# First products of chunk pairs by Strassen's seven block products, token tiles visited there and back

## The chip, the cores and the metric

One core of a Trainium2 chip runs the whole kernel. The metric is device microseconds, the median of three runs. TensorE (PE; its weight loads are PEld) multiplies, VectorE (DVE) and ScalarE (ACT) work elementwise, SyncE (SP) issues most transfers. Matrix results land in PSUM, eight banks of 128 x 512 fp32, and DVE or ACT read them out.

## The reference

Windowed attention with four sink tokens, and then two feed-forward layers on its output:

```
scores = q @ k.T / 8            # kept: keys 0..3, and the 128 keys up to the query's own
x  = softmax(scores) @ v        # 2 x 768 tokens = 1536, 512 wide (8 heads of 64)
h1 = x  @ w_in1                 # 512 -> 2048
x2 = leaky_relu(h1, 0.01) @ w_out1
h2 = x2 @ w_in2
out = silu(h2) @ w_out2         # 1536 x 512
```

The weights come as float64 pairs of words; the kernel turns them into fp32 itself. Each fp32 operand of the feed-forward products is split in two parts, high and low, and a product is the sum of three: high*high, low*high and high*low.

## The kernel before

A recording layer (`Recorder`, L469 is where it issues everything) collects all operations with their dependencies, orders each engine's queue by a planner's costs and due times, and then issues them. The order of every queue is thus fixed when the program is built; on the chip each engine goes down its list and waits where an operand is late. Every row of the profile shows L469, so rows are told apart by tile names.

**Chunks and tiles.** Each layer's 2048 columns are 16 chunks of 128 (chunks 0 to 15 and 16 to 31). The 1536 tokens are three tiles T of 512. For a chunk and a tile the first product `h` (`emit_h`) takes 4 blocks of 128 rows times 3 parts = 12 matmuls of 128x512. ACT and DVE turn `h` into the split pair `gb` (activation, its high part, its low part). The second product (`emit_y`) takes 4 output blocks times 3 = 12 matmuls into the PSUM banks `y0` to `y3`. In layer 2 the activation was a Sigmoid on ACT, a multiplication on DVE, a copy on ACT and a subtraction on DVE.

**Weights.** Each chunk is fetched in two halves (`wr`), and a half is turned into fp32 by one ACT and four DVE operations (`wb`) and split by one ACT and one DVE operation into `w` (a ring of 6 chunks) or `we` (a ring of 4).

**Order.** During the attention, chunks 0 to 5 are worked on half tiles of 256 tokens beside it (`ga`, `ya`). Then come passes of 4 or 6 chunks: in a pass every tile T is visited in the order 0, 1, 2, and its `y` banks add up over the chunks of the pass and are then added into `yp` by DVE. `h` of item f is issued two items ahead of its `y` (`fused_h(f)`, then `fused_y(f - 2)`), so PE alternates 12 matmuls of `h` with 12 of `y`. `h` has two PSUM banks. At the end of layer 1, `yp` is split into `xh` and `xl`, the input of layer 2.

```
for f in range(len(items)):
    ...
    fused_h(f)
    if f >= 2:
        fused_y(f - 2)
```

Of the kernel before, what the change touches and what calls it, by code (L numbers as in the profile page):

```python
# [30 lines left out]
NA, NE = 6, 4  # L31
# [21 lines left out]
def f32(ap):  # L53
    return ap.bitcast(F32)
# [429 lines left out]
def attention_moe(ctx, tc, cfg, ins, out):  # L484
# [22 lines left out]


    chunks = [(w, c) for w in (w1, w2) for c in range(NCH)]
    wt, halves = [], [0]  # L510

    raws = []

    def fetch(n):
        w, c = chunks[n // 2]
        cs = slice(n % 2 * 512, (n % 2 + 1) * 512)
        raws.append(keep.tile([P, 512, 2], U32, "wr", 3))
        R.sync.dma_start(out=raws[n], in_=w[c, :, cs].bitcast(U32).rearrange("p (n t) -> p n t", t=2))

    def load_half(after=None):  # L520

        n = halves[0]
        halves[0] += 1
        while len(raws) < min(n + 1 + FETCH, 2 * len(chunks)):
            fetch(len(raws))
        R.after, R.splitting = after, True
        if n % 2 == 0:
            first = len(wt) % (NA + NE) < NA
            wt.append((keep if first else rest).tile([P, 2, 1024], F32R, "w" if first else "we", NA if first else NE))
        t = wt[-1]  # L530
        cs = slice(n % 2 * 512, n % 2 * 512 + 512)
        lo, hi = raws[n][:, :, 0], raws[n][:, :, 1]
        b = keep.tile([P, 512], U32, "wb", 3)
# [7 lines left out]
        R.scalar.activation(t[:, 0, cs], f32(b), AF.Copy)  # L541
        R.vector.tensor_tensor(t[:, 1, cs], f32(b), f32(t[:, 0, cs]), op=ALU.subtract)
# [13 lines left out]
    def emit_h(gt, t, layer, T, t0, n):  # L556
        hp = ps.tile([P, 512], F32, "h", 2)[:, :n]
        last = KC * 3 - 1
        i = 0
        with R.group():  # L560
            for kc in range(KC):
                for a, b in ((0, xh), (1, xh), (0, xl)):
                    R.tensor.matmul(hp, wi(t, a, kc), b[T][:, kc, t0:t0 + n], start=i == 0, stop=i == last)
                    i += 1
        R.at_h = R.ops[-1]
        g = keep.tile([P, 512], F32, "g", 2)[:, :n]
        if layer == 0:
            R.scalar.activation(gt[:, 0, :], hp, AF.Prelu, alpha=0.01)
            R.scalar.activation(g, hp, AF.Prelu, alpha=0.01)
        else:  # L570
            R.scalar.activation(g, hp, AF.Sigmoid)
            R.vector.tensor_tensor(g, g, hp, op=ALU.mult)
            R.scalar.activation(gt[:, 0, :], g, AF.Copy)
        R.vector.tensor_tensor(gt[:, 1, :], g, f32(gt[:, 0, :]), op=ALU.subtract)

    def emit_y(yps, gt, t, layer, c, first, last, cols=slice(0, 512)):
# [341 lines left out]
    if near:  # L918
        make_mask(0)
        make_mask(1)  # L920

        for t in (*psink, own):
            R.vector.memset(t, 0.0)
        for k in range(2):
            R.vector.memset(own[32 * k:32 * k + 32, k * QB:(k + 1) * QB], 1.0)
        loaded = 2
        load_v(1)
        OFF = 2 * NP + 3
        for b in range(n_slots + 4):
# [12 lines left out]
            while loaded <= b // 2 + (AHEAD if loaded < NP * WHOLE else 1 + b % 2):  # L942
                load_qk(loaded)
                loaded += 1
            if 0 <= b - 1 < n_slots:
                normalise(b - 1)
            if b % 2 == 0 and b >= 4:
                if b % 4 == 2:
                    values(b // 2 - 3)
                load_v(b // 2)  # L950
            if 0 <= b - 2 < n_slots:
                transposes(b - 2)
            if go:
                item_h(m)
                m += 1
    else:
        attend_all()
        while len(wt) < NA:
            load_chunk()


    passes, counts, items, c0 = [], [], [], NA
    for layer, end in ((0, NCH), (1, 2 * NCH)):
        while c0 < end:
            n = min(NE if len(passes) % 2 == 0 else NA, end - c0)
            passes.append(n)
            new = layer == 1 and c0 == NCH

            starts = [min(BESIDE[T], c0) if c0 == NA else c0 for T in range(NT)]
            items += [(layer, c, T, c == starts[T], c == c0 + n - 1, new, c0 + n == end)  # L970
                      for T in range(NT) for c in range(starts[T], c0 + n)]
            counts.append(len(items) - sum(counts))
            c0 += n

    due, n0 = [], 2 * NA
    for n, m_p, nxt in zip(passes, counts, passes[1:] + [0]):
        n0 += 2 * n
        due += [n0 + 2 * nxt * (i + 1) / m_p for i in range(m_p)]
    while m < n_items + 2:
        if halves[0] < 2 * (NA + NE):  # L980
            load_half()
        item_h(m)
        item_y(m - 2)
        m += 1
    yps, fg = [], {}

    def fused_h(f):
        layer, c, T = items[f][:3]
        fg[f] = rest.tile([P, 2, 512], F32R, "gb", 4)
        emit_h(fg[f], wt[c], layer, T, 0, 512)  # L990

    def fused_y(f, banks=None):
        layer, c_w, T, first, last, new, final = items[f]
        gt = fg[f]

        ends = layer == 1 and final and T == NT - 1
        parts = [(c, 0, 512) for c in range(KC - ends)] + ends * [(KC - 1, 0, 256), (KC - 1, 256, 512)]
        if first and banks in (None, [0]):
            yps[:] = [ps.tile([P, 512], F32, "ya0", 1) if o else ps_y.tile([P, 512], F32, f"y{c}") for c, o, _ in parts]
        for k in banks or range(len(parts)):  # L1000
            c, o, e = parts[k]
            cols = slice(o, e)
            yp_k = yps[k][:, :e - o]
            emit_y(yp_k, gt, wt[c_w], layer, c, first, last, cols)
            if not last:
                continue
            part = yp[T][:, c, cols]
            if new:
                R.scalar.activation(part, yp_k, AF.Copy)
            elif not final:  # L1010
                R.vector.tensor_tensor(part, part, yp_k, op=ALU.add)
            elif layer == 0:
                R.vector.tensor_tensor(part, part, yp_k, op=ALU.add)
                R.scalar.activation(xh[T][:, c, :], part, AF.Copy)
                R.vector.tensor_tensor(xl[T][:, c, :], part, f32(xh[T][:, c, :]), op=ALU.subtract)
            else:
                r0 = T * 512 + c * P
                R.vector.tensor_tensor(part, part, yp_k, op=ALU.add)
                (R.scalar if o else R.sync).dma_start(out=out[r0:r0 + P, cols], in_=part)

    for f in range(len(items)):
        while halves[0] < min(2 * len(chunks), due[f]):

            load_half(R.at_h if f else None)
        fused_h(f)
        if f >= 2:
            fused_y(f - 2)

    for k in range(KC + 1):
        for f in (len(items) - 2, len(items) - 1):  # L1030
            fused_y(f, [k])
    R.issue(ctx)


# [87 lines left out]
```

## Time and profile before

| | |
|---|---|
| time, median of 3 runs | 621.07 us (620.93 to 621.36) |
| profiled execution: span from first to last instruction | 619.7 us |
| its own device time | not recorded apart from the span; the median lies 1.4 us above the span |
| PE busy | 609.3 us, 98% |
| DVE busy | 401.3 us, 65% |
| ACT busy | 314.2 us, 51% |
| granted TensorE clock | full in all 40 slices |

A matmul's record is longer than its place in the stream, because matmuls are pipelined: the distance from one start to the next is what counts. The chain of work that ended last is followed back from the last instruction. DVE and ACT records overlap a little in the same way, so both a duration and the start-to-start distance are read below.

### The profile page before, as it was taken

To read this page: it belongs to the slowest core of one execution; us is meant where nothing else is said; L and a number is where in the kernel's file an instruction comes from. 1 tells how busy PE (TensorE), PEld (TensorE's weight loads), DVE (VectorE), ACT (ScalarE), POOL (GpSimd) and SP (SyncE) were. 2 spreads that over 40 slices of the span, in tenths; PEclk is the share of its full clock that TensorE was granted. 3 is DMA by queue.
4 is the path that set the end of the run, shared out by engine and by line. 5 is a ranking of instruction groups with operands and counts; after the bars stand their busy time and mean duration, and the time that the engine had idled before them with its cause. 6 is when DMAs were issued, how large, how long until landed. Compare 5 with 4: busy or idle time off the path is not lost.

```text
span 619.7 us, 9078 instructions
## 1 busy us (share of the span) xinstructions
PE 609.3 (98%) x3374; PEld 517.2 (83%) x3374; DVE 401.3 (65%) x979; ACT 314.2 (51%) x716; POOL 2.9 (0%) x17
## 2 busy tenths in 40 slices
PE   6899999999999999999999999999999999999997
PEld 4788999999988888888888888888888888888886
DVE  6999889888760289721369454986242984268254
ACT  6999899997652155422335434564222442233211
POOL 1000000000000000000000000000000000000000
PEclk9999999999999999999999999999999999999999
DMA  8545554422320033300013200333000231000013
GB/s 298 191 158 179 179 158 140 147 60 82 137 103 0 1 102 138 135 35 0 1 57 113 102 1 31 139 137 102 1 0 1 102 117 54 1 34 2 0 69 135
DMA packets 19340, 53.33 MB, mean 86 GB/s; under 512 B 2144, under 2 KB 6752, under 8 KB 19296
## 3 DMA queue, kind: packets, MB, share of 16 engines
q1 hardware_dynamic: 19152, 52.63, 24.7%
q8 instruction: 26, 0.43, 0.3%
q14 instruction: 18, 0.15, 0.1%
q10 hardware_dynamic: 144, 0.13, 0.1%
HBM read 49.61 MB, written 3.15 MB: 85 GB/s over the span
## 4 chain that ended last, share of the span: by engine, by line
PE 94%; ACT 3%; DVE 1%; DMA 1%; issue 0%; SPq 0%; DVEq 0%
PE h L469 42%; PE y L469 35%; PE ya L469 7%; PE at L469 3%; PE tr L469 3%; PE sc L469 3%; ACT P L469 1%; DMA wr<-in_w 1%; ACT pT L469 0%; ACT wb L469 0%; DVE P L469 0%; SPq L469 0%; DVE by L469 0%; DVE wb L469 0%; ACT w L469 0%
## 5 line engine op out<-in xcount | busy, mean ns | idle before, releaser
L469 PE MATMUL h<-xh,w 128*128 128x512 f32 (+1 forms) x600 | 157.0, 349 | 0.0
L469 PEld LDWEIGHTS h<-xh,w 128*128 128x128 f32 x600 | 104.6, 189 | 14.3 <-issue 0.3
L469 ACT ACTIVATE g<-h 128x512 f32<-128x512 f32 (+1 forms) x111 | 59.8, 539 | 108.5 <-PE h L469 108.4
L469 DVE TENSOR_TENSOR gb<-g,gb 128x512 fp32r<-128x512 f32 x81 | 55.9, 690 | 82.3 <-ACT g L469 64.9
L469 PE MATMUL h<-xl,w 128*128 128x512 f32 (+1 forms) x300 | 103.9, 346 | 0.0
L469 DVE TENSOR_TENSOR g<-g,h 128x512 f32<-128x512 f32 x48 | 32.9, 686 | 90.8 <-ACT g L469 90.7
L469 PE MATMUL h<-xh,we 128*128 128x512 f32 x288 | 88.7, 389 | 0.0
L469 DVE SCALAR_TENSOR_TENSOR wb<-wr,wb 128x512 uint32<-128x512 uint32 x128 | 87.2, 687 | 1.6
L469 PE MATMUL y<-we,gb 128*128 128x512 f32 x288 | 69.2, 389 | 0.0
L469 PE MATMUL y<-w,gb 128*128 128x512 f32 (+1 forms) x288 | 68.2, 387 | 0.0
L469 PEld LDWEIGHTS h<-xh,we 128*128 128x128 f32 x288 | 54.1, 188 | 11.2
L469 PEld LDWEIGHTS y<-we,gb 128*128 128x128 f32 x288 | 54.1, 188 | 11.2
L469 PEld LDWEIGHTS y<-w,gb 128*128 128x128 f32 x288 | 53.8, 188 | 11.0
L469 PEld LDWEIGHTS h<-xl,w 128*128 128x128 f32 x300 | 56.6, 189 | 7.0
L469 PE MATMUL y<-gb,w 128*128 128x512 f32 x252 | 60.5, 389 | 0.0
L469 ACT ACTIVATE P<-P,sm 128x260 f32<-128x260 f32 (+2 forms) x118 | 57.0, 497 | 5.5 <-DVE sm L469 4.8
L469 ACT ACTIVATE gb<-h 128x512 fp32r<-128x512 f32 x33 | 19.7, 598 | 78.7 <-PE h L469 78.7
L469 PE MATMUL h<-xl,we 128*128 128x512 f32 x144 | 56.0, 389 | 0.0
L469 PEld LDWEIGHTS y<-gb,w 128*128 128x128 f32 x252 | 47.3, 188 | 9.8
L469 DVE TENSOR_SCALAR wb<-wb 128x512 uint32<-128x512 uint32 (+1 forms) x128 | 52.7, 422 | 2.7 <-ACT wb L469 1.4
L469 PE MATMUL ya<-ga,w 128*128 128x256 f32 x360 | 50.6, 286 | 0.0
L469 ACT ACTIVATE gb<-g 128x512 fp32r<-128x512 f32 x48 | 30.4, 633 | 35.6 <-DVE g L469 35.6
(78 smaller groups left out, 738.1 us busy)
## 6 DMA issues: line engine op xcount, KB each, us to landing
wr<-in_w SPq DMA_DIRECT2D x64, 512.0 KB, 3.6
qk<-in_qkd SPq DMA_DIRECT2D x12, 644.0 KB, 3.9
v<-in_vd SPq DMA_DIRECT2D x16, 192.0 KB, 3.2
out_y<-yp SPq DMA_DIRECT2D x11, 256.0 KB, 2.0
qk<-in_qkd SPq DMA_DIRECT2D x4, 322.0 KB, 6.0
v<-in_vd SPq DMA_DIRECT2D x8, 128.0 KB, 4.8
qkh<-in_qkd SPq DMA_DIRECT2D x4, 256.0 KB, 6.2
qk<-in_qkd SPq DMA_DIRECT2D x3, 256.0 KB, 4.1
```

The source lines that it names most:

```text
L469: getattr(eng, name)(*[_real(x) for x in a], **{k: _real(x) for k, x in kw.items()})
```

## The change

In 11 of the 16 pairs of neighbouring chunks (four in layer 1, from chunk 8; seven in layer 2, from chunk 18) the first products of two chunks over the tiles T = 0 and T = 1 are made together. Before they were 4 x 12 = 48 matmuls. Now the input is taken as 2x2 blocks (tile by half of the 512 columns), the two chunks' weights as 2x2 blocks (half by chunk), and Winograd's form of Strassen's rule makes seven block products of 6 matmuls, 42 in all (`product`). The tile T = 2 goes as before (`h_plain`).

The rule needs sums of input blocks once per layer (`combos`: tiles `S0` to `S2` and, in place, half of `xh[1]`, `xl[1]`), sums of weight blocks once per pair (in `load_half`: four subtractions of 128x256 on DVE, then two splits into `wx`), and three additions of results per pair (`sum_of` on DVE, with three copies out of PSUM, `held`, on ACT). Products are accumulated in the PSUM banks `ya0` (bank A), `ya1` (bank C) and one of the two `h` banks (bank B).

Three further parts: the second products of the two chunks of a pair are issued one after the other for each output block (`y_pair`), and `yp` is added to after each pair and not after each pass, except that a tile which is last in one pair is first in the next (order 0, 1, 2, then 2, 1, 0), so its banks stay open over both. Layer 2's activation is Silu twice on ACT and a subtraction on DVE. The ring `we` is gone; `w` keeps 6 chunks, and the loads of chunks 6 to 9 move from the end of the attention into the first items after it. Each layer starts with a few items as before (`plain_run`), and the last two of them hand their `y` to the first pair (`todo`, `other`).

```
+    def split(hi, lo, b):
+        R.scalar.activation(hi, b, AF.Copy)
+        R.vector.tensor_tensor(lo, b, f32(hi), op=ALU.subtract)
...
+        if h == 0 and c >= NA and c % 2 and c - 1 not in plain:
+            b0, b1 = f32(bits[c - 1]), f32(b)
+            u, v = slice(0, 256), slice(256, 512)
+            for o, x, y in ((b0[:, u], b1[:, u], b0[:, u]), (b1[:, u], b1[:, v], b1[:, u]),
+                            (b1[:, v], b1[:, v], b0[:, u]), (b0[:, v], b0[:, v], b1[:, v])):
+                R.vector.tensor_tensor(o, x, y, op=ALU.subtract)
+            wx[c - 1] = [rest.tile([P, 2, 512], F32R, "wx", 2) for k in range(2)]
+            for x, y in zip(wx[c - 1], (b0, b1)):
+                split(x[:, 0, :], x[:, 1, :], y)
...
-            R.scalar.activation(g, hp, AF.Sigmoid)
-            R.vector.tensor_tensor(g, g, hp, op=ALU.mult)
-            R.scalar.activation(gt[:, 0, :], g, AF.Copy)
+        f, kw = (AF.Prelu, dict(alpha=0.01)) if layer == 0 else (AF.Silu, {})
+        R.scalar.activation(gt[:, 0, :], h, f, **kw)
+        R.scalar.activation(g, h, f, **kw)
         R.vector.tensor_tensor(gt[:, 1, :], g, f32(gt[:, 0, :]), op=ALU.subtract)
...
+    def plain_run(layer, items, n_loads, at):
+        todo, S = [], None
+        for f, (c, T, first, last) in enumerate(items):
+            loads(f < n_loads)
+            h_plain(c, T)
+            todo.append((c, T, first, last))
+            if f == at:
+                S = combos(layer)
+            if f >= 2:
+                y_parts(*todo.pop(0))
+        return todo, S
...
+    def product(bank, x, w, start):
...
+        with R.group():
+            for k in range(2):
+                for a, b in ((0, 0), (1, 0), (0, 1)):
+                    R.tensor.matmul(bank, w(a, k), x[b][:, k, :], start=start and i == 0, stop=start and i == 5,
+                                    skip_group_check=not start)
...
+        A = bank("ya0")
+        product(A, x(0, 0), W(c, 0), True)
+        m1 = held(A)
+        B = bank("h", 2)
+        product(B, x(0, 1), W(c, 1), True)
+        sum_of(c, 0, m1, B)
+        loads(1)
+        other()
+        C = bank("ya1")
+        product(C, S1, X(t1, 0), True)
+        m5 = held(C, "s5", 1)
+        other()
+        h_plain(c, 2)
+        product(A, S2, X(t2, 1), False)
+        m16 = held(A)
+        product(C, S4, W(c + 1, 1), False)
+        sum_of(c + 1, 0, m16, C)
+        loads(1)
+        h_plain(c + 1, 2)
+        product(A, S3, X(t2, 0), False)
+        sum_of(c + 1, 1, m5, A)
+        T = order[0]
+        y_pair(c, T, first(T), last(T), range(2))
+        product(A, x(1, 1), X(t1, 1), False)
+        activate(new_g(c, 1), A, layer)
+        loads(1)
+        y_pair(c, T, first(T), last(T), range(2, KC))
+        y_pair(c, order[1], first(order[1]), last(order[1]))
+        loads(1)
+        y_pair(c, order[2], first(order[2]), last(order[2]))
```

How the queues stand now, at the places of which the prediction speaks. In PE's queue, in the middle of a stretch, before: one item's `y`, the next item's `h` (chunk 11, tile 1).

```order
L469 MATMUL y0_4_3531<-gb_23_3535,w_8_3082 128x512 x3
L469 MATMUL y1_4_3540<-gb_23_3535,w_8_3082 128x512 x3
L469 MATMUL y2_4_3545<-gb_23_3535,w_8_3082 128x512 x3
L469 MATMUL y3_4_3549<-gb_23_3535,w_8_3082 128x512 x3
L469 MATMUL h_60_3613<-xh1_0_589,w_11_3291 128x512 x2
L469 MATMUL h_60_3613<-xl1_0_609,w_11_3291 128x512
L469 MATMUL h_60_3613<-xh1_0_589,w_11_3291 128x512 x2
L469 MATMUL h_60_3613<-xl1_0_609,w_11_3291 128x512
```

PE now, in the pair of chunks 20 and 21 whose first tile in turn is T = 2; these rows follow the `h` of chunk 21 and tile 2, from which `gb_48` is made. `ya0` is bank A.

```order
L469 MATMUL ya0_13_4498<-xh1_0_589,wx_11_4492 128x512 x2
L469 MATMUL ya0_13_4498<-xl1_0_609,wx_11_4492 128x512
L469 MATMUL ya0_13_4498<-xh1_0_589,wx_11_4492 128x512 x2
L469 MATMUL ya0_13_4498<-xl1_0_609,wx_11_4492 128x512
L469 MATMUL y0_16_4550<-w_20_4352,gb_46_4630 128x512 x3
L469 MATMUL y1_16_4558<-w_20_4352,gb_46_4630 128x512 x3
L469 MATMUL y0_16_4550<-w_21_4420,gb_48_4678 128x512 x3
L469 MATMUL y1_16_4558<-w_21_4420,gb_48_4678 128x512 x3
L469 MATMUL ya0_13_4498<-xh1_0_589,wx_10_4472 128x512 x2
L469 MATMUL ya0_13_4498<-xl1_0_609,wx_10_4472 128x512
L469 MATMUL ya0_13_4498<-xh1_0_589,wx_10_4472 128x512 x2
L469 MATMUL ya0_13_4498<-xl1_0_609,wx_10_4472 128x512
```

Between an `h` and the second product that reads it stood two `y` and two `h`, 48 matmuls; now 12 lie between the `h` of `gb_48` and its first use. Bank A is filled again 12 matmuls after its last filling.

In ACT's queue at the change from layer 1 to layer 2, where the table of functions is loaded, before (`we_7` is chunk 15, `h_67` layer 2's first):

```order
L469 ACTIVATE we_6_3806<-wb_37_3845 128x512
L469 ACTIVATE wb_39_3891<-wr_39_3808 128x512
L469 ACTIVATE we_7_3895<-wb_38_3847 128x512
L469 ACTIVATE gb_32_3903<-h_66_3876 128x512
L469 ACTIVATE g_62_3906<-h_66_3876 128x512
L469 ACTIVATE we_7_3895<-wb_39_3891 128x512
L469 ACT_TABLE_LOAD
L469 ACTIVATE g_63_3939<-h_67_3923 128x512
L469 ACTIVATE gb_33_3948<-g_63_3939 128x512
```

ACT now at the same place (`xh0` is layer 2's input of tile 0, `w_17` chunk 17's weights, `h_55` layer 2's first `h`):

```order
L469 ACTIVATE xh1_0_589<-yp1_0_1315 128x512
L469 ACTIVATE xh0_0_318<-yp0_0_838 128x512 x2
L469 ACTIVATE wb_45_4046<-wr_37_3999 128x512
L469 ACTIVATE xh0_0_318<-yp0_0_838 128x512 x2
L469 ACTIVATE w_17_3997<-wb_43_3919 128x512
L469 ACT_TABLE_LOAD
L469 ACTIVATE gb_33_4072<-h_55_4033 128x512
L469 ACTIVATE g_59_4074<-h_55_4033 128x512
L469 ACTIVATE gb_34_4092<-h_56_4054 128x512
```

The split of tile 0's input and of chunk 17's second half now stand ahead of the load; before they stood far from it. PE's queue has three `h` in a row there (`h_55`, `h_56`, `h_57`), where before it went on alternating.

DVE at the same place, before, from layer 2's first `h` (`g_63`) on back to chunk 15's weights:

```order
L469 SCALAR_TENSOR_TENSOR wb_39_3891<-wr_39_3808,wb_39_3891 128x512 x2
L469 TENSOR_TENSOR gb_32_3903<-g_62_3906,gb_32_3903 128x512
L469 TENSOR_TENSOR we_7_3895<-wb_39_3891,we_7_3895 128x512
L469 TENSOR_TENSOR g_63_3939<-g_63_3939,h_67_3923 128x512
L469 TENSOR_TENSOR gb_33_3948<-g_63_3939,gb_33_3948 128x512
```

DVE now, up to the low part of layer 2's first `gb`:

```order
L469 TENSOR_TENSOR yp0_0_838<-yp0_0_838,y0_11_3987 128x512
L469 TENSOR_TENSOR yp0_0_838<-yp0_0_838,y1_11_4003 128x512
L469 TENSOR_TENSOR yp0_0_838<-yp0_0_838,y2_11_4012 128x512
L469 TENSOR_SCALAR wb_43_3919<-wb_43_3919 128x512
L469 TENSOR_TENSOR yp0_0_838<-yp0_0_838,y3_11_4021 128x512
L469 SCALAR_TENSOR_TENSOR wb_43_3919<-wr_35_3828,wb_43_3919 128x512
L469 TENSOR_TENSOR xl0_0_353<-yp0_0_838,xh0_0_318 128x512
L469 SCALAR_TENSOR_TENSOR wb_43_3919<-wr_35_3828,wb_43_3919 128x512
L469 TENSOR_TENSOR xl0_0_353<-yp0_0_838,xh0_0_318 128x512 x2
L469 TENSOR_TENSOR w_17_3997<-wb_43_3919,w_17_3997 128x512
L469 TENSOR_TENSOR gb_33_4072<-g_59_4074,gb_33_4072 128x512
```

These are the last of a run of 12 additions into `yp` and 12 subtractions for `xl`, all three tiles, with chunk 17's weights between them; before, each tile's four and four stood 6 items apart.

## Rows read from the trace of the kernel before

**Rows 1.** The page: span, busy time by engine, granted clock in 40 slices.
```profile
span 619.7 us, 9078 instructions
PE 609.3 (98%) x3374; PEld 517.2 (83%) x3374; DVE 401.3 (65%) x979; ACT 314.2 (51%) x716; POOL 2.9 (0%) x17
PEclk9999999999999999999999999999999999999999
```

**Rows 2.** Busy time in stretches: PE, PEld, DVE, ACT, POOL, then clock, DMA share, GB/s.
```profile
0.00:50.00 50.00, 42.90 (x328) 33.78 (x329) 44.59 (x193) 43.82 (x139) 2.89 (x17) 1.00 0.61 208
...
300.00:350.00 50.00, 50.00 (x222) 41.40 (x222) 31.90 (x58) 21.10 (x38) 0.00 (x0) 1.00 0.23 78
...
600.00:620.00 20.00, 16.48 (x79) 13.70 (x77) 9.73 (x16) 2.46 (x4) 0.00 (x0) 1.00 0.43 157
```

**Rows 3.** The chain that ended last, in order of time: start, us, engine, tile.
```profile
268.25 2.72 PE h L469 x12
270.97 2.72 PE y L469 x12
...
371.61 2.72 PE h L469 x12
```

**Rows 4.** The timeline behind one `h` of layer 1: start us, us, engine, operation [idle before].
```profile
281.46 0.39 PE L469 MATMUL h<-xl,w 128*128 128x512 f32 x1
...
281.88 0.60 ACT L469 ACTIVATE gb<-h 128x512 fp32r<-128x512 f32 x1 [4.35 <-PE h L469]
282.38 0.59 ACT L469 ACTIVATE g<-h 128x512 f32<-128x512 f32 x1
283.00 0.69 DVE L469 TENSOR_TENSOR gb<-g,gb 128x512 fp32r<-128x512 f32 x1 [4.75 <-ACT g L469]
```

**Rows 5.** The timeline of DVE where operations follow each other without a wait.
```profile
296.45 2.49 DVE L469 TENSOR_TENSOR xl<-yp,xh 128x512 fp32r<-128x512 f32 x4
...
316.25 0.88 DVE L469 TENSOR_SCALAR wb<-wb 128x512 f32<-128x512 f32 x2
...
317.17 1.42 DVE L469 SCALAR_TENSOR_TENSOR wb<-wr,wb 128x512 uint32<-128x512 uint32 x2
```

**Rows 6.** Groups by operation and shape: busy us, mean ns of one, idle before.
```profile
L469 PEld LDWEIGHTS h<-xh,w 128*128 128x128 f32 x600 | 104.6, 189 | 14.3 <-issue 0.3
L469 DVE TENSOR_TENSOR gb<-g,gb 128x512 fp32r<-128x512 f32 x81 | 55.9, 690 | 82.3 <-ACT g L469 64.9 <-ACT gb L469 17.2
L469 ACT ACTIVATE g<-h 128x512 f32<-128x512 f32 x81 | 48.2, 596 | 108.5 <-PE h L469 108.4
L469 ACT ACTIVATE wb<-wr 128x512 f32<-128x512 f32 x64 | 41.9, 669 | 4.4 <-DMA wr<-in_w 4.3
L469 DVE TENSOR_TENSOR yp<-yp,y 128x512 f32<-128x512 f32 x59 | 37.5, 682 | 10.2 <-PE y L469 10.2
L469 DVE TENSOR_TENSOR g<-g,h 128x512 f32<-128x512 f32 x48 | 32.9, 686 | 90.8 <-ACT g L469 90.7
L469 DVE TENSOR_TENSOR ga<-g,ga 128x256 fp32r<-128x256 f32 x30 | 12.6, 421 | 6.0 <-ACT g L469 6.0
```

**Rows 7.** The timeline at the change from layer 1 to layer 2.
```profile
352.40 2.88 PE L469 MATMUL y<-gb,w 128*128 128x512 f32 x12
...
352.65 1.28 ACT L469 ACT_TABLE_LOAD   x1 [3.88 <-PE h L469]
353.94 0.60 ACT L469 ACTIVATE g<-h 128x512 f32<-128x512 f32 x1
...
354.57 0.69 DVE L469 TENSOR_TENSOR g<-g,h 128x512 f32<-128x512 f32 x1 [5.00 <-ACT g L469]
```

**Rows 8.** DMA issues: size, median us to landing.
```profile
wr<-in_w SPq DMA_DIRECT2D x64, 512.0 KB, 3.6
```

**Rows 9.** The timeline of the last microseconds.
```profile
616.51 0.42 DVE L469 TENSOR_TENSOR yp<-yp,ya 128x256 f32<-128x256 f32 x1 [0.30 <-PE ya L469]
616.97 0.37 ACTq L469 DMA_DIRECT2D out_y<-yp  x1
```

More of the change, by code (lines that the diff above doesn't have):

```diff
@@ L523, in load_half @@
         halves[0] += 1
[L524 removed]
+        while len(raws) < min(n + 1 + FETCH, len(hv)):
             fetch(len(raws))
         R.after, R.splitting = after, True
[L527 to L531, printed above, removed]
+        c, h = hv[n]
+        if c not in wt:
+            wt[c] = keep.tile([P, 2, 1024], F32R, "w", NA)
+        t = wt[c]
+        cs = slice(h * 512, h * 512 + 512)
         lo, hi = raws[n][:, :, 0], raws[n][:, :, 1]
[L533 removed]
+        b = bits[c] = keep.tile([P, 512], U32, "wb", 3)
         R.scalar.activation(f32(b), f32(hi), AF.Abs)
@@ L957, in attention_moe @@
         attend_all()
[L958 to L978, printed above, removed]
+        while halves[0] < 2 * NA:
+            load_half()
     while m < n_items + 2:
-        if halves[0] < 2 * (NA + NE):
-            load_half()
         item_h(m)
@@ L984, in attention_moe @@
         m += 1
[L985 to L1001, printed above, removed]
+    gts, yps, opened = {}, {}, set()
@@ new lines, in attention_moe, with loads, new_g, h_plain @@
+    END = 2 * NCH - 1
+    def loads(n):
+        for _ in range(n):
+            if halves[0] < len(hv):
+                load_half(R.at_h)
+    def new_g(c, T):
+        gts[c, T] = rest.tile([P, 2, 512], F32R, "gb", 6)
+        return gts[c, T]
+    def h_plain(c, T):
+        emit_h(new_g(c, T), wt[c], c // NCH, T, 0, 512)
+    def parts_of(c, T):
+        ends = c >= END - 1 and T == NT - 1
+        return [(k, 0, 512) for k in range(KC - ends)] + ends * [(KC - 1, 0, 256), (KC - 1, 256, 512)]
@@ L1002, in fused_y, with y_parts @@
+    def y_parts(c, T, first, last, ks=None):
+        layer = c // NCH
+        parts = parts_of(c, T)
+        for k in ks or range(len(parts)):
+            k0, o, e = parts[k]
+            if first:
+                yps[T, k] = ps.tile([P, 512], F32, "ya0", 1) if o else ps_y.tile([P, 512], F32, f"y{k}")
             cols = slice(o, e)
-            yp_k = yps[k][:, :e - o]
-            emit_y(yp_k, gt, wt[c_w], layer, c, first, last, cols)
+            yp_k = yps[T, k][:, :e - o]
+            emit_y(yp_k, gts[c, T], wt[c], layer, k0, first, last, cols)
@@ L1005, in fused_y @@
             if not last:
                 continue
-            part = yp[T][:, c, cols]
-            if new:
+            part = yp[T][:, k0, cols]
+            if (layer, T) not in opened and layer == 1:
                 R.scalar.activation(part, yp_k, AF.Copy)
-            elif not final:
+            else:
                 R.vector.tensor_tensor(part, part, yp_k, op=ALU.add)
[L1012 to L1015, printed above, removed]
-            else:
-                r0 = T * 512 + c * P
-                R.vector.tensor_tensor(part, part, yp_k, op=ALU.add)
+            if c % NCH < NCH - 1:
+                continue
@@ L1019, in fused_y @@
+            if layer == 0:
+                R.scalar.activation(xh[T][:, k0, :], part, AF.Copy)
+                R.vector.tensor_tensor(xl[T][:, k0, :], part, f32(xh[T][:, k0, :]), op=ALU.subtract)
+            else:
+                r0 = T * 512 + k0 * P
                 (R.scalar if o else R.sync).dma_start(out=out[r0:r0 + P, cols], in_=part)
[L1021 to L1027, printed above, removed]
@@ L1029, in attention_moe, with y_pair @@
-    for k in range(KC + 1):
-        for f in (len(items) - 2, len(items) - 1):
-            fused_y(f, [k])
+        if last and len(parts) - 1 in (ks or range(len(parts))):
+            opened.add((layer, T))
+    def y_pair(c, T, first, last, ks=None):
+        for k in ks or range(len(parts_of(c, T))):
+            for d in range(2):
+                y_parts(c + d, T, first and d == 0, last and d == 1, [k])
+    def plain_run(layer, items, n_loads, at):
[9 more added lines that the diff above has]
+        return todo, S
@@ new lines, in product, with pair_run, other, held @@
+    def product(bank, x, w, start):
+        i = 0
+        with R.group():
+            for k in range(2):
+                for a, b in ((0, 0), (1, 0), (0, 1)):
+                    R.tensor.matmul(bank, w(a, k), x[b][:, k, :], start=start and i == 0, stop=start and i == 5,
+                                    skip_group_check=not start)
+                    i += 1
+        R.at_h = R.ops[-1]
+    def pair_run(c, S, todo, order, first, last):
+        layer = c // NCH
+        S1, S2, S3, S4 = S
+        W = lambda c, q: lambda a, k: wi(wt[c], a, 2 * q + k)
+        t1, t2 = wx[c]
+        X = lambda t, q: lambda a, k: t[:, a, q * 256 + k * P:q * 256 + (k + 1) * P]
+        x = lambda T, q: (xh[T][:, 2 * q:2 * q + 2], xl[T][:, 2 * q:2 * q + 2])
+        bank = lambda t, n=1: ps.tile([P, 512], F32, t, n)
+        def other():
+            if todo:
+                y_parts(*todo.pop(0))
+        def held(a, tag="g", bufs=2):
+            g = (keep if tag == "g" else rest).tile([P, 512], F32, tag, bufs)
+            R.scalar.activation(g, a, AF.Copy)
+            return g
+        def sum_of(c, T, g, b):
+            R.vector.tensor_tensor(g, g, b, op=ALU.add)
+            activate(new_g(c, T), g, layer, g=g)
+        A = bank("ya0")
[28 more added lines that the diff above has]
+        y_pair(c, order[2], first(order[2]), last(order[2]))
@@ L1032, in attention_moe @@
+    layer_run(1, [(NCH + d, T, d == 0, d == 1 and T != 0) for T in (2, 1, 0) for d in range(2)], 4, 3, NCH + 2, 2 * NCH)
     R.issue(ctx)
```

61 lines of the change are left out of this document (49 added, 12 removed).

## The prediction

> **What bounds the kernel now.** I read the page first. PE is busy in 609.3 of 619.7 us, DVE in 65%, ACT in 51%, at full clock (2.4 GHz) in all slices [rows 1]. By stretches, what PE does not fill lies in the first 50 us (7.1 us) and the last 20 (3.5 us); in the stretch from 300 to 350 us PE has no gap while DVE works 31.9 of 50 us [rows 2]. The chain of waits agrees: it runs from one group of 12 matmuls to the next, each 2.72 us, with nothing of another engine between them; from 268.25 to 371.61 us there are 39 such rows in a line [rows 3]. So one 128x512 matmul costs 2.72 / 12 = 226.7 ns of the end, whatever its own record says (389 ns long, because they overlap), and a matmul less is worth that, as long as DVE and ACT stay out of the way. They do so with ease now: what `h` gives is ready 283.69 - 281.85 = 1.84 us after the last matmul of `h` [rows 4], and is wanted 48 matmuls, 10.9 us, later.
>
> **What is removed.** 11 pairs times (48 - 42) = 66 matmuls of 128x512. Counted over PE's whole queue there are 1938 of that shape before and 1872 now, and 764 of 128x256 in both: 66 fewer and no other change. 66 x 0.2267 = 14.96 us. Each product has the same shapes and the same order of weight loads (one per matmul, as now), so I take the same distance for it. Here a rule speaks against the size: the Trainium skill, TensorE: Matmul & The Clock Gate, section Back-to-back issue gap, gives about 131 ns per matmul of 512 columns in a stream of weight loads and matmuls; by it 66 matmuls would be worth 8.6 us (an estimate), and the time 614.2. The trace differs: its stream steps by 226.7 ns [rows 3].
>
> **What is added to DVE and ACT.** By counts of the queues, DVE has 623 operations of 128x512 for 532 and 108 of 128x256 for 64. At about 0.69 us and 0.42 us [rows 6] that is 91 x 0.69 + 44 x 0.42 = 81 us more: from 401 to 482 us, of some 606. In the sum is the loss of the 48 multiplications of the Sigmoid form (32.9 us) and the growth of the additions into `yp` from 59 to 103. ACT has 71 more, 71 x 0.60 = 43 us, 357 in all. None of it stands on the path by itself; what matters is the pair, where it is densest.
>
> A pair takes PE 42 + 24 + 72 = 138 matmuls, 31.3 us. DVE's share, by distances from start to start: operations in a row step by about 0.61 us (2.49 us for 4), two that depend on each other by 0.73 (1.42 less 0.69), two TENSOR_SCALAR take 0.88 us [rows 5]. Four half loads: 4 x (0.88 + 1.42 + 0.62) = 11.7 us; weight sums 4 x 0.42 + 2 x 0.62 = 2.9; three result sums 1.9; six low parts of `gb` 3.7; eight additions into `yp` 4.9. Together 25.1 us, 80% of the pair. It fits, with 6 us to spare, if the waits inside it don't add up.
>
> So I walked the queues through a pair with these durations. The tightest place is the one shown in the order of PE: `gb_48` is wanted 12 matmuls, 2.72 us, after its `h`, its low part only as third matmul, at 3.17 us; with free engines it is ready after 1.84 us [rows 4], and DVE, which finishes the loads' and the weight sums' steps ahead of it, comes to it some 0.6 us later: 0.7 us to spare. Bank A must be read by `sum_of` before its next filling, 2.72 us after its last one; DVE ends that at 1.7 us: 1.0 us to spare. The sum for chunk c + 1, tile 0 has 2.72 + 1.36 us until its use, and needs 0.7 (DVE) + 0.6 + 0.5 (ACT) + 0.7 (DVE) = 2.5 us. The last activation from bank A has 18 matmuls, 4.1 us, until its use and about 1 us to spare, as DVE comes to it late. So I put the eleven pairs at no stall; the cover is the PE work named, and if it is gone each miss costs its own tenths, eleven times over or five or six (by the order of the tiles).
>
> The sums of inputs are 24 DVE operations in layer 1 and 16 in layer 2, 15 and 10 us; in layer 1 they begin before the last plain items end and DVE has no gap for some 40 us, but the first product with `S0` stands 36 matmuls, 8.2 us, behind the last plain `h`, and by the walk has 3 us to spare. The loads of chunks 6 to 9, now later, are due 22 us after chunk 0's slot is free, and a half takes about 3.6 us of transfer [rows 8], 0.67 for ACT [rows 6] and 4 us of DVE and ACT steps. SP's queue holds only these loads, each issued two ahead; I cost them at nothing. The tail is the same list, two last chunks and then the last quarter tile and its store [rows 9]: nothing.
>
> **The change of layers.** Here a stall comes in. In the profile PE goes through the change without a gap: ACT had been idle for 3.9 us, loads the table as soon as `h` ends (352.65 us), for 1.28 us, and its answer is not urgent, as PE has a `y` to do next [rows 7]. Now PE has three `h` in a row there. The third needs the bank of the first, 12 matmuls (2.72 us) after the first has ended. After the first ends, ACT has the table load and two activations: 1.28 + 0.5 + 0.6 = 2.4 us. That alone would just fit. But ACT's queue has the split of chunk 17's second half ahead of the load, and that waits for DVE, which has 32 operations in one run from the first addition of tile 2 on (12 additions, 12 subtractions and chunk 17's steps), before it was idle 5.0 us there [rows 7]. 28 x 0.61 + 4 x 0.44 = 18.8 us, about 19.3 with the dependent steps. Counting from the start of the six matmuls that fill bank A ahead of the last pair's first `y` in layer 1, the run starts at 3.7 us and ends at 23.0; ACT splits until 23.65, loads until 24.95, and has read the bank at 26.05. PE would want it at 24.48, after 1.36 + 17.68 us of products and `y` and 5.44 us of two `h`, and gets it at about 26.2: a stall of 1.7 us. Bounds: if DVE keeps up with PE, the load begins at 22.6 and the stall is 0.6; nothing if the load is done before the wait; 2.5 if DVE's run is 4% slower. I take 1.7, which is the walk's own value.
>
> The Trainium skill, ScalarE: Activation LUTs, section What ACT_TABLE_LOAD costs and its terms, puts a switch of tables at about 2.7 us; by it the stall would be 3.1 us and the sum 609.2. The trace's load took 1.28 us [rows 7], and I go by it.
>
> Silu does not occur in the trace. Prelu and Sigmoid share one row, 596 ns [rows 6]; I take the same for Silu. The bounds are 0.6 and twice that: at 1.2 us the place of `gb_48` above would be late by 0.5 us, in about seven pairs, once or twice each, 3.5 to 7 us. A gain below nothing is excluded: these steps are only waited for.
>
> **Sum.** Against the profiled execution: span 619.7 - 14.96 + 1.7 = 606.4 us; what lies around the span (1.4 us to the median, no own time is recorded) stays. Against the median: 621.07 - 14.96 + 1.7 = 607.8 us.
>
> **Rivals.**
> - *Dense with no stall at the change.* DVE keeps up: 606.1 us. For it: one load is only 1.28 us; against it: the run of 32 operations. It lies in the likeliest case's own range, 606.0 to 609.2.
> - *Handoffs late in each pair.* 0.2 to 0.8 us in each of eleven pairs, from bank A's reader or a low part: 2.2 to 8.8 us, so 610.0 to 616.6. For it: slack fell from about 9 us to under 1, and DVE is 80% busy; against it: the walk finds every one covered. Silu at twice its price would come out here too.
> - *The switch of tables costs more than its record.* If ACT must also run dry and fill again, one activation's 0.6 us on either side, the stall is 2.9 us: 609.0. Against it: the next activation starts 0.01 us behind the load [rows 7]. The page on ScalarE named above says the like.
> - *A matmul less is worth less than its step*, where the stream could go at its weight loads' 189 ns [rows 6]: 66 x 0.189 = 12.5 us, 610.3. Against it: 39 groups of 12 in a line at 2.72 us [rows 3], whichever operands they take. The page on TensorE named above goes further the same way.
> - *Slower: DVE sets the period of a pair.* A pair has some 43 DVE operations. If each pays 0.2 us of waiting on ACT or PE, because low parts, sums and weight steps stand in one queue, the pair lasts 25.1 + 8.6 = 33.7 us where PE needs 31.3: 11 x 2.4 = 26.4 us, 634 us. It decides from (14.96 - 1.7) / 11 = 1.2 us a pair on. For it: every low part in the trace waits for ACT (64.9 us in 81) [rows 6]; against it: those waits are for work that came late, on an engine with nothing else to do.
> - *It doesn't do what it says*, saving fewer matmuls: excluded by the counts.
>
> **Chances.** Likeliest case 0.62, late handoffs 0.24 (their lower part, to 612.5, 0.14), tables 0.03, cheaper matmuls 0.03, slower by DVE 0.05, faster still (below 605.5) 0.03. The range takes in the first, the lower part of the second, tables and cheaper matmuls, 0.82: 605.5 to 612.5. 0.2%, 1.24 us, is what a measurement of this kernel can tell from no change: faster (below 619.8) 0.94, the same 0.02, slower (above 622.3) 0.04.
>
> **What would show it.** PE's matmuls of 128x512 fall by 66 and its busy time by about 15 us, with 226.7 ns a step in the pairs; DVE near 480 us and about 80% in the pair stretches; ACT near 357 us. A single new gap of PE, about 1.7 us, before the third `h` of layer 2, whose releaser is ACT and behind it a table load. Wrong would be: PE's waits for `gb` or bank A that come back in every pair, a Silu of more than 0.65 us, or PE's step longer than 227 ns in the products.

## The result, and the profile after

| | before | after |
|---|---|---|
| time, median | 621.0 us (620.84 to 621.36, 4 runs) | 607.45 us (606.98 to 608.09, 4 runs) |
| span of the profiled execution | 619.7 us | 605.3 us (its own time: 607.04) |
| PE, DVE, ACT busy | 609.3, 401.3, 314.2 us | 595.7, 473.3, 351.3 us |

The ratio is 0.978, 95% interval 0.9767 to 0.9794: 13.6 us faster. The forecast was 607.8 us, range 605.5 to 612.5.

The page of the changed kernel, beside [rows 1]; the last number of an engine counts its instructions.

```profile
span 605.3 us, 9097 instructions
PE 595.7 (98%) x3308; PEld 505.4 (84%) x3308; DVE 473.3 (78%) x1114; ACT 351.3 (58%) x787; POOL 2.9 (0%) x17
PEclk9999999999999999999999999999999999999999
```

PE has 3374 - 3308 = 66 matmuls less, at the same full clock. The added work is all there, 72 us on DVE and 37 us on ACT, and the span shrank all the same: it lies beside PE. By stretches, beside [rows 2] (two pairs of chunks last 62.56 us; the first row is layer 1, the third layer 2, the second holds the change of layers):

```profile
242.60:305.16 62.56, 62.56 (x277) 51.80 (x276) 48.00 (x87) 28.70 (x51) 0.00 (x0) 1.00 0.21 68
...
350.00:400.00 50.00, 49.68 (x219) 40.77 (x219) 43.09 (x78) 33.17 (x60) 0.00 (x0) 1.00 0.22 74
...
436.08:498.64 62.56, 62.56 (x278) 51.80 (x277) 48.01 (x87) 28.70 (x50) 0.00 (x0) 1.00 0.21 68
```

In the pairs PE is never without work, and DVE works 48.0 / 2 = 24.0 us in each pair of 31.28 us, 77%. The chain of waits reads the same, beside [rows 3]: one pair of layer 2, from one run of 48 `y` matmuls to the next.

```profile
436.08 10.88 PE y L469 x48
446.96 1.36 PE h L469 x6
448.32 1.36 PE ya L469 x6
449.68 2.72 PE h L469 x12
452.40 2.72 PE ya L469 x12
455.12 2.72 PE h L469 x12
457.84 1.36 PE ya L469 x6
459.20 2.72 PE y L469 x12
461.92 1.36 PE ya L469 x6
463.28 2.72 PE y L469 x12
466.00 1.36 PE ya L469 x6
467.36 10.88 PE y L469 x48
```

A product of six takes 1.36 us and a plain `h` 2.72: one step, 226.7 ns, for all. 467.36 - 436.08 = 31.28 us is 138 such steps, with nothing between them. PE's waits from behind the first `y` of layer 1 to 600 us, in layer 2's last items, are one row (us in total, times, longest):

```profile
PE h L469 <- ACT g L469: 0.3, 1, 0.3
```

It is the gap that was forecast, before the third `h` of layer 2. The chain around it, beside [rows 7]:

```profile
350.58 0.60 DVE wb L469
351.18 0.60 DVE xl L469
351.78 0.62 DVE wb L469
352.40 0.02 issue
352.42 0.63 ACT w L469
353.06 0.02 issue
353.07 1.28 ACT L469
354.36 0.01 issue
354.37 0.60 ACT gb L469
354.96 0.50 ACT g L469
355.46 0.04 issue
355.51 3.06 PE h L469 x12
```

Read it upwards: PE's `h` waits for the bank that ACT reads (`g`); that stands behind the table load (the ACT row without a tile name), that behind the split of chunk 17 (`w`), and that waits for DVE, which has gone from step to step at 0.60 us. The third `h` should have started 2 x 2.72 us after the first, which began at 349.59 by the timeline, so at 355.03; it started at 355.51, 0.48 us late, and ran slower than its step at first. The `y` behind it started at 358.40 by the timeline, and 349.59 + 3 x 2.72 is 357.75: 0.65 us late in all.

The groups by operation and shape, beside [rows 6]:

```profile
L469 DVE TENSOR_TENSOR gb<-g,gb 128x512 fp32r<-128x512 f32 x70 | 48.2, 689 | 26.2 <-ACT g L469 25.4
L469 ACT ACTIVATE g<-h 128x512 f32<-128x512 f32 x37 | 22.0, 595 | 0.0
```

Silu, in the last row together with Prelu, is as long as the functions before. The waits of `gb` for ACT fell from 64.9 us in 81 operations to 25.4 in 70, as DVE now has other work in that time. The weights' transfer [rows 8] now lands after 3.8 us, and the last addition [rows 9] begins 3.2 us before the span's end, as before.

### The profile page after: what moved, and what is told of

Same layout as the page of the kernel before. It is cut to its first block, busy times and chain, and to the rows that moved or that the text cites. A ratio compares the mean times of both kernels' runs of the same rounds, so it can differ in the third digit from the quotient of the medians.

```text
span 605.3 us, 9097 instructions
## 1 busy us (share of the span) xinstructions
PE 595.7 (98%) x3308; PEld 505.4 (84%) x3308; DVE 473.3 (78%) x1114; ACT 351.3 (58%) x787; POOL 2.9 (0%) x17
## 4 chain that ended last, share of the span: by engine, by line
PE 89%; DVE 5%; ACT 3%; DMA 2%; issue 0%; SPq 0%; DVEq 0%
PE y L469 34%; PE h L469 24%; PE ya L469 21%; PE at L469 4%; PE tr L469 3%; PE sc L469 3%; ACT P L469 1%; DVE yp L469 1%; DVE wb L469 1%; DVE xl L469 1%; DMA wr<-in_w 1%; DMA sr<-in_vs 1%; DVE P L469 1%; ACT pT L469 0%; ACT wb L469 0%
## 5 line engine op out<-in xcount | busy, mean ns | idle before, releaser
L469 PE MATMUL y<-w,gb 128*128 128x512 f32 (+1 forms) x576 | 134.1, 388 | 0.0
L469 PEld LDWEIGHTS y<-w,gb 128*128 128x128 f32 x576 | 107.8, 188 | 22.3
L469 PE MATMUL y<-gb,w 128*128 128x512 f32 x396 | 93.0, 389 | 0.0
L469 PEld LDWEIGHTS y<-gb,w 128*128 128x128 f32 x396 | 74.3, 188 | 15.4
L469 DVE TENSOR_TENSOR yp<-yp,y 128x512 f32<-128x512 f32 x104 | 69.3, 678 | 7.1 <-PE y L469 7.0
L469 DVE TENSOR_TENSOR gb<-g,gb 128x512 fp32r<-128x512 f32 x70 | 48.2, 689 | 26.2 <-ACT g L469 25.4
L469 ACT ACTIVATE w<-wb 128x512 fp32r<-128x512 f32 x64 | 40.4, 633 | 36.8 <-DVE wb L469 36.5
L469 DVE TENSOR_TENSOR w<-wb,w 128x512 fp32r<-128x512 f32 x64 | 43.9, 687 | 6.5 <-ACT w L469 5.8
L469 PEld LDWEIGHTS ya<-ga,w 128*128 128x128 f32 x360 | 45.7, 190 | 2.1 <-issue 1.7
L469 ACT ACTIVATE wb<-wr 128x512 f32<-128x512 f32 x64 | 42.7, 668 | 4.3 <-DVE wx L469 3.0
L469 DVE CUSTOM_DVE_ANT_0 P<-sc,mask 128x260 f32<-128x260 f32 (+2 forms) x90 | 33.0, 399 | 3.3 <-PE sc L469 3.2
```

What stands on the lines that cost most here:

```text
L469: getattr(eng, name)(*[_real(x) for x in a], **{k: _real(x) for k, x in kw.items()})
```

## The experiments

Theory A, mine: a matmul less is worth one step of 226.7 ns, the pairs are covered, and the only new stall is at the change of layers. Theory B: part of the gain is from the other parts of the change (turning back, Silu, loads moved), so that a matmul less is worth less than its step, or DVE's work costs something in every pair.

The executions differ before the pairs begin, where all kernels from the change on do nearly the same work: the first `y` of layer 1 starts at 182.6 to 184.2 us. So the table also gives the distances from that `y` to layer 2's first `h`, from there to the `y` after the three `h`, and from there to the span's end, all from the timelines. The page gives a span to 0.1 us, so the last two columns are good to 0.05 us and their differences to 0.1; the other columns are good to 0.01.

| kernel | time, median (range) | ratio to before (95%) | first `y` at | to `h` | three `h` | to the end | first `y` to end |
|---|---|---|---|---|---|---|---|
| before | 621.07 | | 183.76 | | | | 435.94 |
| after | 607.45 (606.98 to 608.09) | 0.978 (0.9767 to 0.9794) | 183.67 | 165.92 | 8.81 | 246.90 | 421.63 |
| e1_again | 606.84 (606.66 to 607.26) | 0.9766 (0.9744 to 0.9788) | 183.38 | 165.92 | 8.80 | 246.90 | 421.62 |
| e2_third_bank | 606.43 (605.39 to 607.35) | 0.9757 (0.9734 to 0.9781) | 182.61 | 165.92 | 8.16 | 246.91 | 420.99 |
| e3_no_products | 621.2 (620.7 to 622.0) | 0.9998 (0.9985 to 1.001) | 183.63 | | | | 435.97 |
| e4_layer2_only | 611.53 (611.05 to 611.92) | 0.9841 (0.9818 to 0.9863) | 183.74 | | | | 426.36 |
| e5_no_turning | 607.55 (606.82 to 607.92) | 0.9777 (0.976 to 0.9793) | 184.18 | 165.92 | 9.19 | 246.91 | 422.02 |
| e6_sigmoid | 607.25 (606.91 to 607.44) | 0.9775 (0.9761 to 0.979) | 183.53 | 165.92 | 9.03 | 247.12 | 422.07 |
| e7_dve_plus6 | 606.17 (605.92 to 607.46) | 0.9763 (0.9748 to 0.9777) | 183.09 | 166.03 | 8.16 | 246.82 | 421.01 |
| e8_dve_plus12 | 611.19 (610.75 to 611.62) | 0.9839 (0.9824 to 0.9854) | 183.12 | 169.37 | 9.06 | 247.35 | 425.78 |

**e1_again.** The changed kernel once more, beside the next three on one chip.

> The changed kernel once more, unchanged, so that the others are compared with it in the same stretch of time. Its four times lay at 607.0 and 608.0, two each. Theory A (the time is PE's stream of matmuls; everything added to DVE and ACT is hidden, except one stall of 0.65 us before the third first product of layer 2): 607.0 to 608.1 again, ratio to before 0.977 to 0.979. Theory B (the other parts of the change, turning back and Silu, bring a good part of the gain, and the block products lose part of theirs in waits): the same here.

Measured 606.84 us. The two profiled executions of this kernel, 0.3 us apart in span, differ only ahead of the pairs (183.38 against 183.67) and agree behind, within what the columns can tell. A difference of half a microsecond between two medians is therefore not read as an effect below; one in the last three columns is, where it is larger than they can err.

**e2_third_bank.** The third `h` of layer 2 gets a bank that is free, so it waits for nobody:

```
-    def h_plain(c, T):
-        emit_h(new_g(c, T), wt[c], c // NCH, T, 0, 512)
+    def h_plain(c, T, tag="h"):
+        emit_h(new_g(c, T), wt[c], c // NCH, T, 0, 512, tag)
...
-            h_plain(c, T)
+            h_plain(c, T, "ya0" if layer == 1 and f == 2 else "h")
```

> One edit: the third first product of layer 2 goes into the free bank ya0, so it need not wait until ACT, behind the table load, has read the first product's bank. Theory A: the 0.32 us gap and the slower matmuls behind it go, 0.65 us less: about 606.8, with PE without a gap from 186 us to the end. If the stall only moves to the next wait (the second product that reads the first gb, one group of 12 later): no change, 607.4, and a gap of PE before y in place of the one before h.

ACT's and PE's timeline at that place, with the third `h` in `ya`:

```profile
351.36 0.63 ACT L469 ACTIVATE w<-wb 128x512 fp32r<-128x512 f32 x1 [1.09 <-DVE wb L469]
352.01 1.28 ACT L469 ACT_TABLE_LOAD   x1
353.31 0.60 ACT L469 ACTIVATE gb<-h 128x512 fp32r<-128x512 f32 x1
...
353.80 0.59 ACT L469 ACTIVATE g<-h 128x512 f32<-128x512 f32 x1
353.97 0.62 PE L469 MATMUL ya<-xh,w 128*128 128x512 f32 x2
```

ACT is as late as in the change (it frees the bank at 354.39, PE would want it at 353.97), but PE starts on time. The three `h` take 8.16 us, exactly 36 steps, and the whole kernel from the first `y` on 420.99: 0.64 us less. That is the stall, and all of it. The medians differ by as little as 0.4 us from e1_again, and the range here (605.39 to 607.35) takes in all of its, so the trace decides here and not the time. No version is shorter from the first `y` on; e7_dve_plus6 below comes level (421.01).

**e3_no_products.** All first products plain, with neither sums of inputs nor of weights; order of the tiles, Silu, the ring of weights and the moved loads of chunks 6 to 9 stay as changed. The second products go item by item again, as before, and not for two chunks together (`y_pair`, but for the last two items of a layer), and the later weights are loaded at fixed items (not shown).

```
-        if h == 0 and c >= NA and c % 2 and c - 1 not in plain:
+        if False:
...
-            pair_run(c, S, todo, order, lambda T: T != order[0], lambda T: done or T != order[2])
+            items += [(c + d, T, T != order[0] and d == 0, (done or T != order[2]) and d == 1)
+                      for T in order for d in range(2)]
```

> All of the change but the seven products: first products as before for all tiles, no sums of inputs, weights or results. Turning back, Silu, the ring of six chunks and the later loads stay. PE has 1938 matmuls of 128x512 again. Theory A: 607.45 + 66 x 0.2267 = 622.4 us, within 1 us, that is no better than before (621.0), and PE without gaps. Theory B: clearly below before, 612 to 618, since turning back and Silu would keep their part.

It takes the time of before, ratio 0.9998 (0.9985 to 1.001), and 435.97 against 435.94 us from the first `y` on, with no wait of PE in either. So theory B's first half falls: the other parts that stay bring nothing. Against e2_third_bank, which has the products and no stall, it is 435.97 - 420.99 = 14.98 us longer, for 66 matmuls: 227 ns each, to 1.5 ns. A matmul less is worth its step. The spans of the two are 619.6 and 603.6 us; the first `y` of layer 1, here and in e2_third_bank:

```profile
183.63 2.88 PE L469 MATMUL y<-gb,w 128*128 128x512 f32 x12
...
182.61 2.88 PE L469 MATMUL y<-gb,w 128*128 128x512 f32 x12
```

**e4_layer2_only.** Products in the seven pairs of layer 2 alone; layer 1 goes item by item, `h` and `y` in turn (its other lines are not shown).

```
-        if h == 0 and c >= NA and c % 2 and c - 1 not in plain:
+        if h == 0 and c >= NCH and c % 2 and c - 1 not in plain:
```

> The seven products in layer 2 only (seven pairs), layer 1 with plain first products and no sums of inputs. Theory A: each pair is worth 6 x 0.2267 = 1.36 us, so 607.45 + 4 x 1.36 = 612.9 us. Theory B: not in proportion; if the gain comes from the first pairs or from the other parts, 608 to 611, if layer 1 loses by its sums of inputs (24 DVE operations), below 612.

Measured 611.53 us. From the first `y` on it is 426.36 - 420.99 = 5.37 us longer than e2_third_bank, for 4 x 6 = 24 matmuls: 224 ns each, to 4 ns. Against e3_no_products it is 435.97 - 426.36 = 9.61 us shorter, for 7 x 6 = 42: 229 ns, to 2.4. So a pair is worth 1.34 us in layer 1 and 1.37 in layer 2, the same within what the spans can tell. The stall at the change of layers is gone here too. Three `h` still stand in a row there, but in ACT's queue the split of `w` comes at 361.71 us by the timeline, behind the table load at 357.14.

**e5_no_turning.** Tiles always in the order 0, 1, 2, and every bank added into `yp` after each pair.

```
-            pair_run(c, S, todo, order, lambda T: T != order[0], lambda T: done or T != order[2])
-            order = order[::-1]
+            pair_run(c, S, todo, order, lambda T: T != order[0] or c > c0, lambda T: True)
```

> One edit: every pair visits the tiles in the order 0, 1, 2, and every tile's banks are read out after each pair. DVE gets four more additions of about 0.6 us per pair, 2.4 us, about 88% of a pair in place of 80%. PE's matmuls are the same. Theory A: 607 to 608.5, since 6 us a pair were free. Theory B (turning back brings a good part): 3 to 10 us slower than the changed kernel, 611 to 617.

DVE works more in a pair, PE does not notice (two pairs, layer 2):

```profile
436.08:498.64 62.56, 62.56 (x277) 51.80 (x277) 53.34 (x96) 28.85 (x50) 0.00 (x0) 1.00 0.19 68
```

26.7 us a pair for 24.0. The only loss is at the change of layers, where the three `h` take 0.38 us more than in the change. It is another wait than there: the first `h` has to wait for the last low parts of its own input, which DVE makes too late for it.

```profile
PE h L469 <- DVE xl L469: 0.4, 1, 0.4
```

In the pairs turning back brings nothing, since DVE has time to spare. With the tiles always from 0 on, the place of `gb_48`, where tile 2 comes first, does not occur in this kernel.

**e6_sigmoid.** Layer 2's activation in its former form, with two more steps behind `h` in line.

```
+        if layer == 0:
...
+        else:
+            g = keep.tile([P, 512], F32, "g", 2)[:, :n]
+            R.scalar.activation(g, h, AF.Sigmoid)
+            R.vector.tensor_tensor(g, g, h, op=ALU.mult)
+            R.scalar.activation(gt[:, 0, :], g, AF.Copy)
```

> One edit: layer 2's activation in the form of before (Sigmoid on ACT, multiplication on DVE, copy on ACT, subtraction on DVE). From first product to low part 3.2 us in place of 1.84, and six more DVE operations per pair, 3.6 us, about 92% of a pair. PE's order is set anew by the planner with this known. Theory A: PE stays dense as long as the planner finds matmuls to put between, 607 to 611. Theory B (Silu is a part of the gain): 612 to 620, with PE waits for gb in the pairs of layer 2.

422.07 us from the first `y` on, 0.44 more than the change: 0.22 in the three `h`, some 0.2 behind them. PE's waits are again a single row, before the third `h`:

```profile
PE h L469 <- DVE g L469: 0.6, 1, 0.6
```

In the pairs nothing waits, though DVE has 27.4 us (54.81 in two pairs) and `gb` comes later by a multiplication and a copy. That does not try the place that the walk had called tight: with the longer activation known to it, the planner put 24 matmuls of PE between the `h` of `gb_48` and its first use in layer 2, and not 12, by issuing all four `y` of the even chunk first. So, with the queues ordered anew, Silu's work saved is worth 0.4 us at most; in the order of the change it was not tried. Of what lies behind the three `h`, PE's stream from the `y` there to its last matmul is 243.69 us long and 243.67 in the change; the rest, some 0.2 us, comes after PE's last matmul, where the last items stand in another order.

**e7_dve_plus6 and e8_dve_plus12.** What each DVE operation costs when the pair gets denser: the low parts of weights and of their sums are computed twice, or three times, 6 or 12 more operations of 128x512 a pair. The edit of the first; the second has 2 for 1.

```
-    def split(hi, lo, b):
+    def split(hi, lo, b, again=0):
         R.scalar.activation(hi, b, AF.Copy)
-        R.vector.tensor_tensor(lo, b, f32(hi), op=ALU.subtract)
+        for _ in range(1 + again):
+            R.vector.tensor_tensor(lo, b, f32(hi), op=ALU.subtract)
...
+        split(t[:, 0, cs], t[:, 1, cs], f32(b), 1 if c >= NA else 0)
```

> The subtraction that makes the low part of each weight half and each weight sum is done twice in chunks 6 to 31, with the same result: six more DVE operations of about 0.60 us per pair, 3.6 us, about 92% of a pair's 31.3 us. Theory A: DVE still fits, 607 to 609. The rival that DVE already sets the period of some pairs: 11 x 3.6 = 40 us slower, or a good part of it, 615 and more.

> The same subtraction three times: twelve more DVE operations per pair, 7.2 us. DVE then has 25.1 + 7.2 = 32.3 us by the sum of its work where PE needs 31.3. Theory A: DVE becomes the bound, at least 11 x 1.0 = 11 us slower and up to 20 with its waits: 618 to 628, with PE gaps in every pair. If DVE's real work in a pair is less than 24 us: 608 to 612.

With 6 more, DVE in two pairs of each layer, and PE full:

```profile
436.08:498.64 62.56, 62.56 (x278) 51.80 (x277) 55.47 (x99) 28.81 (x50) 0.00 (x0) 1.00 0.19 68
242.60:305.16 62.56, 62.56 (x278) 51.80 (x277) 58.30 (x106) 28.47 (x50) 0.00 (x0) 1.00 0.21 73
```

It is not slower but 0.62 us shorter than the change from the first `y` on, and that by the way: the planner, with other costs, put ACT's split of chunk 17 behind the table load. Its timeline:

```profile
351.44 1.28 ACT L469 ACT_TABLE_LOAD   x1
...
352.73 0.60 ACT L469 ACTIVATE gb<-h 128x512 fp32r<-128x512 f32 x1
...
353.23 0.59 ACT L469 ACTIVATE g<-h 128x512 f32<-128x512 f32 x1
...
353.70 0.63 ACT L469 ACTIVATE w<-wb 128x512 fp32r<-128x512 f32 x1
```

The load no longer waits for DVE, the three `h` take 8.16 us, and the stall is gone as in e2_third_bank, without another bank; e4_layer2_only, where the split also stands behind the load, agrees. So the load, as long as ever, costs nothing in itself here; what made the stall was the split that stood ahead of it in ACT's queue.

With 12 more, DVE is full:

```profile
436.08:498.64 62.56, 62.56 (x278) 51.80 (x277) 61.81 (x112) 29.21 (x51) 0.00 (x0) 1.00 0.20 70
242.60:305.16 62.56, 62.36 (x276) 51.30 (x275) 62.30 (x114) 28.84 (x51) 0.00 (x0) 1.00 0.20 68
```

31.15 us of 31.28 in a pair of layer 1, and PE's waits from the first `y` on are three rows:

```profile
PE y L469 <- DVE yp L469: 2.1, 3, 1.0
PE h L469 <- ACT g L469: 0.6, 1, 0.6
PE y L469 <- DVE gb L469: 0.4, 2, 0.2
```

Against e7_dve_plus6 it is 4.77 us longer: 3.34 in layer 1 (2.06 us of PE's time between 211.3 and 242.6 us alone, the first pair, where the sums of inputs stand in the queue too and DVE already works 29.68 of 31.30 us in the change), 0.90 at the change of layers, 0.53 in layer 2. The pairs by themselves still fit, but for two waits of 0.2 us. I had expected 618 us or more, from 25.1 us a pair and 0.60 us an operation, with 608 to 612 if DVE's real work was under 24 us; it is 24.0, so it was the pair that I had put too high. By these numbers the limit of a pair is (31.28 - 24.0) / 0.60 = 12 operations, and e8 stands on it; the first pair of layer 1 gives way sooner.

## Why the prediction was right

**Removed: 66 matmuls by 226.7 ns.** Right in count and price: 14.98 us, to 0.1, against 14.96 (e3_no_products less e2_third_bank). The rival that a matmul is worth less than its step falls.

The figure of the Trainium skill weighed beside it (TensorE: Matmul & The Clock Gate, section Back-to-back issue gap), about 131 ns, would have given 614.2 us (an estimate). The measured 227 ns decides.

**Added: DVE and ACT beside PE.** Right that it is hidden. The size was over: 482 and 357 us forecast, 473.3 and 351.3 found. For these sums I had priced operations at their record, 0.69 us; in a full queue the next starts after 0.60, and busy time counts the overlap once. The pair was priced by distances from start to start, and there it is 24.0 us against 25.1. The rival that DVE sets the period needed 1.2 us of loss a pair; it has none, and e8_dve_plus12 shows how far off that is: 12 operations in a regular pair, not a few.

**The pairs at no stall.** Right: not one wait in eleven pairs. The tight places held, but with less to spare than the walk gave them. The pair that follows the one shown above begins with tile 0; in the next, chunks 24 and 25, tile 2 comes first again:

```profile
490.32 2.88 PE L469 MATMUL y<-w,gb 128*128 128x512 f32 x12
491.03 0.68 DVE L469 TENSOR_TENSOR gb<-g,gb 128x512 fp32r<-128x512 f32 x1
491.63 0.68 DVE L469 TENSOR_TENSOR s<-s,ya 128x512 f32<-128x512 f32 x1
...
493.04 0.62 PE L469 MATMUL ya<-xh,wx 128*128 128x512 f32 x2
```

The low part (here of `gb_60`, which stands as `gb_48` did) is first read by the ninth of the twelve `y`, at 490.32 + 8 x 0.2267 = 492.13 us, and is done at 491.71: 0.42 us to spare for 0.7, and 0.41 and 0.42 in the other two such pairs of layer 2. Bank A is read by 492.31 and filled again at 493.04: 0.73 for 1.0. So the mechanism was right, and in these pairs the two margins were put too high by about 0.3 us. Of the four experiments that press the pairs, only the two with more work for DVE have `gb_48` in its place: e5_no_turning has no such pair, and in e6_sigmoid it stands elsewhere. In e7_dve_plus6, where the planner has DVE's queue in another order, nothing waits.

**The change of layers.** The mechanism was right in each of its links, and the size is the term that failed: 1.7 us forecast, 0.65 found. Behind DVE's end all went as walked: split, load and the bank read, 3.05 us forecast, 355.46 - 352.40 = 3.06 found. But DVE's run ended at 21.85 us after the walk's origin (330.55 by the timeline) and not at 23.0. It began at 3.60 (3.7 forecast) and lasted 18.25 us and not 19.3:

```profile
334.15:352.40 18.25, 18.25 (x82) 15.10 (x81) 18.25 (x33) 11.35 (x20) 0.00 (x0) 1.00 0.08 29
```

DVE, the third pair of numbers, had no gap in it: 33 operations in 18.25 us, the last of them begun at 352.31. My 0.5 us for dependent steps was wrong: the steps of `wb` have another operation between them in the chain above, and each starts 0.60 us behind it. The four TENSOR_SCALAR operations took about 0.33 us each from start to start, and I had put 0.44, 0.4 us too much in all; 0.61 a step was 0.01 too much, 28 times. The lower bound that I had worked out, "if DVE keeps up with PE", put the load at 22.6 us and the stall at 0.6: the load began at 353.07 - 330.55 = 22.52. The rival of a dearer switch of tables falls: the next activation starts 0.01 us behind the load's 1.28 us, as before.

**Silu** at 596 ns: right, 595 found (the mean of Silu and Prelu).

**The sum.** From the first `y` of layer 1 to the end the change took 435.94 - 421.63 = 14.31 us off, and 14.96 less the stall's 0.65 is 14.31: the two terms explain it whole. With the stall as measured the median would have been 621.07 - 14.96 + 0.65 = 606.8 us. The medians were 607.45 and 606.84, the profiled execution 607.04; the difference is of the size of the spread ahead of the pairs, but its cause was not followed. What lies around the span was not 1.4 us but 607.04 - 605.3 = 1.74, and 1.72 to 1.85 in the experiments' profiled executions; by that the profiled execution of before was itself some 0.4 us longer than its median (an estimate; its own time was not recorded). The 1.05 us too much for the stall and the spread partly cancel, so that 607.8 against 607.45 is in part luck: the forecast looks closer than its terms were.

## What to carry to other kernels

Where one engine goes without a gap and the chain shows it step after step, work taken from it is worth its start-to-start distance. Work put on the others was free here until their busy time in a stretch, counted at their own start-to-start distance, nearly filled it; the stretch to look at is the densest one, here the first pair of layer 1 and not a regular pair. A margin is to be read from the timeline of the kernel that has it: an experiment whose queues are ordered anew may not hold the place that it was meant to try. New stalls are to be looked for where the regular pattern breaks (a change of layers, a table load), in what stands ahead of the late instruction on its own queue: in e7_dve_plus6 the whole wait was gone with one split behind the load. To see effects of half a microsecond, compare distances between two marks inside the traces and not medians of whole runs.

## What was not expected of the hardware

- DVE operations of 128x512 with two tiles to read (TENSOR_TENSOR and SCALAR_TENSOR_TENSOR) start every 0.60 us in a full queue, though a record is 0.68 to 0.69 us long; a TENSOR_SCALAR gives way to the next after 0.33 to 0.34, with a record of 0.41 or 0.42. Two that depend on each other lose nothing if one stands between them (`wb` at 350.58 and 351.78 in the chain, with `xl` at 351.18).
- A gap in PE's stream costs more than its length. Before the third `h` the view of waits shows 0.3 us, but the work behind came 0.65 us late: matmul records are longer than their steps, so the first 0.16 us of a gap is hidden under the last record, and the twelve matmuls after it took 2.89 us to the next start and not 2.72, at full granted clock in that stretch. In e8_dve_plus12, likewise, 0.6 us of wait cost 0.90. Why the first steps are slower the runs don't show.
- Nearly equal work ahead of the pairs ended at 182.61 to 184.18 us in the nine executions from the change on. The first transfer of the chain took 5.10 us in the earliest and 5.75 in the latest, but 5.79 and 5.83 in two that lie between (e3_no_products, e4_layer2_only), so it is not the whole cause; the rest was not followed.
